# Sending half of a triangular solve's products to the other half of PSUM, in a fused delta-rule attention and MLP kernel

## The chip, the cores and the metric

The kernel runs on one core of a Trainium2 chip. The metric is the device time of one execution in microseconds; the times below are medians over several runs. A core has a matrix engine (TensorE, "PE"), three others that compute (VectorE "DVE", ScalarE "ACT", GpSimd "POOL"), a fifth that here only issues transfers (SyncE, "SP"), and 16 DMA engines. Each engine works through its own list of instructions in order; semaphores make one wait for another. Matrix products land in PSUM, which has 128 partitions and eight banks; DVE and ACT read them from there.

## The reference

There are 4 x 8 = 32 heads, 768 tokens and a head dimension of 48. Each head runs a delta rule over the tokens; the result goes through a two-layer MLP (384 to 2048 to 384) with a tanh Gelu.

```
k_n = k / (norm(k) + 1e-6)
for t in range(S):
    y[t]  = q[t] @ state
    state = state + beta[t] * outer(k_n[t], v[t] - k_n[t] @ state)
x = y with the heads side by side              # 3072 x 384
out = gelu_tanh(x @ w_in) @ w_out
```

## The kernel before

The 768 tokens are cut into 12 chunks of 64. Within a chunk the rule is a triangular system, so the work of a chunk c has these stages, each for all 32 heads at once. A "pair" p is two heads: one lies in partitions 0 to 63 of every tile, the other in 64 to 127, and there are 16 pairs.

- `prep(c)` squares the keys (`sq`), sums them (`ss`, L603) and forms 1/norm (`rn`). For chunks 0 to 3 the root is taken on ACT. From chunk 4 on it is taken for two chunks at once on DVE by a bit trick and three Newton steps (`norms`, L621 to L628: 12 small instructions). `prep2` multiplies keys by `rn` (`Kn`, POOL or DVE), transposes them on PE (L680) and copies the result into `KQT`. `prepq` does the same for the queries, two chunks at a time (L648).
- `gram` forms K K^T and K Q^T (`G`, `DT`). `own` forms the 16 x 16 diagonal blocks of K K^T, and `solve` inverts them on POOL (chunk 0: on DVE), in pairs of chunks from 2 on. `back` (L806) transposes the inverses into `TB`; `exp` spreads them over zero-padded tiles: `DI` (block diagonal) and `WB`.
- `inverse(c)` makes the inverse `TT` of the 64 x 64 triangle from the four diagonal blocks, by Horner's scheme. First `ET` = a product of `G` and `WB` ("WB,G" in the profile), masked. Then for k = 1, 2, 3: a product of `ET` with `DI` (k = 1) or with `TT` so far (k = 2, 3), 64 - 16k columns wide, and an addition of `DI` into `TT` on DVE. In the profile the products are "DI,ET" (64x48) and "TT,ET" (64x32, 64x16). Each is 32 matmuls with a 64 x 64 stationary tile, one for each head.
- `state(c)` computes v minus what the state already says (`R`), `U` = `TT` times `R`, the new state `S` and the chunk's rows of x.
- `mlp(t)` works on token tiles: chunks 0 to 3 are a tile each, then two chunks make a tile (eight tiles). Its first layer goes in blocks of one PSUM bank ("x,W"), each followed by a Gelu on ACT into `gT`; its second layer is "W,gT", evicted to `osb` and sent out.

All matmuls of attention and MLP stand on L267 (`f_mms`), all DVE and POOL two-operand operations on L251 (`f_tt`), copies on L256 (`f_cp`), most of ACT's on L260 (`f_act`), all DMA issues on L275 (`f_dma`).

A product with a 64 x 64 tile can read from either half of the partitions and write to either half. In the product WB,G of chunks 2 on, even pairs write to the half that they read from, and odd pairs to the other half and another bank (`flip` in `prod`). In the products of the loop over k, every pair writes to the half that it reads from.

Nothing is scheduled at run time or by a planner in this file. The string `ORDER` gives every operation, by its number in the order of creation and the letter of the engine that is to run it (v, a, g, p, s for DVE, ACT, POOL, PE, SP), in one sequence; each engine's list is its part of it, and an operation that can run on several engines is put on one by that letter. Words such as `w12.5` are 12 filler matmuls ("spins", L414) into bank 5. The string `BANK` gives the PSUM bank of each product. `BANKS` limits which banks a kind may have: 0 to 5 for attention ("t"), 6 and 7 for the MLP ("f"), any for the first chunks and the last tile ("l"). A product waits for every user of its bank's last tile.

Of the kernel before, what the change touches and what calls it, by code (L numbers as in the profile page):

```python
# [19 lines left out]
v33 v10 s56 v3 w6.7 p61 v36 v37 v9 v38 s51 v42 v7 v40 s52 a82 g84 v63 s60 a24 g20 v85 g17 a29 v39 v62 a30 a31 v83 a32  # L20
a23 v67 a86 s59 v70 a87 v64 v88 s57 a97 g75 v89 v65 g81 s58 w12.5 p91 v66 a98 p99 g90 v44 v92 g77 w1.4 p93 a103 v68
p100 v94 g72 g76 a101 s96 p152 v104 g74 v153 g73 a105 w1.7 p181 a106 a182 v107 v154 g108 v156 v155 g69 w8.3 p109 v157
v158 v159 a110 v160 v183 g80 s141 a102 v161 w4.5 p264 v162 v163 v164 p178 v265 a179 v165 g266 v166 a117 v167 v168 v169
v170 a25 a28 g267 a27 v171 g268 g269 v172 g270 g271 v173 g272 g273 v174 g274 g275 v175 g276 g277 v176 a185 g278 g279
s95 a184 v177 w29.3 p191 g280 p301 g281 v192 g282 a187 p189 v186 g283 v190 g284 a188 w1.5 p195 g285 v118 p193 g286
a196 g287 a194 p199 v71 g288 v180 p197 g289 a200 g78 a119 p203 v198 a120 g290 a205 p201 v121 g291 v204 v122 g79 a202
p209 a302 p206 g292 g293 s147 v207 a210 g294 g295 a125 v208 s140 v211 g296 w3.5 p215 v303 p216 g297 p217 s146 p304
v218 a219 p212 p123 v126 a305 g299 v298 a127 a128 v129 a133 v306 g130 v300 s115 v124 a213 s113 g400 w12.7 p131 v308
a309 s116 p398 v132 a311 s114 g603 v214 p399 a250 s111 p314 v401 a310 s112 a315 v251 s144 g402 s142 a375 v307 s143
g403 g404 w10.6 p312 v376 a135 s145 g405 p224 g406 s262 g407 p226 v377 a225 g408 v378 s263 v379 p328 a134 g409 v380  # L30
p228 v381 g410 v382 a313 s151 g411 v329 p136 g412 p137 s150 a229 g413 v383 p316 v138 p318 g414 s149 a317 v384 g415
p438 a227 v385 s223 p230 g416 v386 v139 a439 g417 s222 p232 a231 v387 g418 s148 v388 p320 a233 g419 v389 p459 v319
g390 s220 p234 a460 v440 s221 p322 a235 v321 p456 v461 p324 g420 a323 s396 a457 g393 p326 p441 s397 v327 a519 p236
v325 v458 p333 a442 g421 v520 p238 g422 a334 p391 g423 a253 v443 g424 p330 g425 a239 v331 p338 g426 p394 a252 v332
g427 v335 p339 v392 p340 g428 p341 a578 s259 p342 g429 p240 g430 v344 s260 g431 a343 g433 v579 a395 s258 p254 a237
g432 v580 p601 s345 v437 p602 s261 a444 v434 p241 s346 v462 s347 v604 p255 s348 a242 p349 s436 v256 g605 p351 a350
s435 v581 p644 v582 a352 p466 s531 v583 g521 p353 v584 a645 v585 s532 v445 p245 g522 a354 v646 a257 g606 v586 v587
g607 p355 g608 v464 a467 g609 p336 v588 v446 p448 g610 v337 p246 g611 a449 g612 v589 g613 v463 p523 g614 v590 a356
v591 p474 g615 v592 a247 p450 g690 a447 p357 v451 p359 v475 g593 p524 a360 p452 v525 a358 p468 g616 v453 a526 s599
p361 g596 v469 s600 p454 a362 p363 s527 v455 g617 v691 p476 s530 g618 p470 a477 g619 p480 s529 p594 g620 a364 p481  # L40
s528 g621 p478 a482 g622 p365 v479 s483 g623 a771 g624 s489 v471 p366 g625 s491 a595 v772 g626 s488 g627 g628 p533
a243 v773 s490 p662 v774 g629 p597 a244 v775 s492 g630 v776 p370 g631 a598 v777 s487 v778 g632 v779 g633 v780 s703
a367 g634 p371 v781 g636 v782 a692 s702 v783 v784 v785 g635 p794 v534 a372 a663 p795 v640 g786 a465 p493 v647 p495
v664 a494 g693 p472 v797 a496 p497 s792 g883 p499 v473 a498 s793 v637 p535 v648 s638 g796 p501 a536 v884 s699 p539
a502 p540 p641 g798 s486 v541 p694 a642 s639 p503 a500 v643 s700 g799 p695 a504 g800 p505 v696 g801 s548 p507 a506
s546 v697 p537 a665 s547 p651 g789 p659 v652 p509 s701 a508 s550 v538 a660 g802 p790 s549 g803 a374 p510 v661 g804
s698 a958 g805 v791 s551 g806 a249 v649 p837 g807 p669 v959 s484 p653 a248 g808 s485 p514 g809 a838 v654 g810 a668
g811 v670 a511 p515 g812 g813 v667 v839 g814 p552 g815 v960 a516 v961 p655 g816 v962 a553 p834 g817 v656 p677 a835
g818 p554 v963 g819 a650 v678 p556 g820 a555 g821 p657 v836 a557 g822 p558 v658 a886 g823 v666 g824 p679 g825 a559
p683 p671 g826 a680 g827 p560 g828 v672 p681 a561 p562 v682 g829 p673 a563 v830 p684 p704 v674 s832 a685 p564 v705  # L50
s545 p675 a565 s831 p852 v676 a369 p566 v964 s542 a853 v965 p710 v966 s544 p706 v967 a567 p568 v968 s543 v969 a707
v970 v841 a368 v854 p711 p855 v971 a712 p569 v860 v972 v859 g973 a856 v833 s719 p787 a373 v842 s720 p573 v857 a858
g885 s717 s721 p974 v840 a517 s722 p708 v788 p862 a570 g976 p574 s718 v863 a512 s688 v709 s687 g981 p864 a575 p977
s689 a576 v865 p887 s686 g1133 p888 v975 p723 v889 p844 a724 p725 v845 a861 p727 a843 v978 a726 p979 v890 a728 p980
p846 v982 p729 p731 v847 g983 a730 p1019 a732 p866 p1022 g984 v867 p848 g985 a1023 g986 p733 v849 g987 p735 g988 v1024
g989 p1131 a736 g990 g991 p1132 a734 g992 a1020 p737 g993 v1021 p739 g994 a738 g995 v1134 p870 a740 g996 p741 g997
p743 v871 a742 g998 g999 p850 a518 g1000 p868 a744 g1001 p745 v869 g1002 v851 p747 g1003 a746 g1004 p872 a748 p876
g1005 p749 a873 g1006 g1007 p751 a750 g1008 p874 g1009 a752 p877 g1010 v875 p753 a878 g1011 g1012 p1037 g1013 p891
a754 p755 v892 a577 g1135 a513 v1015 p897 a571 p893 s1016 g1014 p756 v894 a1038 s716 s715 g1136 v1018 g1137 p898 p1040
s714 g1138 a899 p759 g1139 s1017 v757 g1140 a1041 g1141 v1039 s713 p760 g1142 a572 v1043 s907 g1143 a1025 v1042 g1144  # L60
s906 p763 g1145 v1044 s904 v1026 g1146 a758 s908 g1147 v1045 v761 p1171 g1148 s905 p1029 a1172 p764 g1149 s909 a1028
g1150 v1173 s903 g1151 v1030 p767 g1152 a765 s881 g1153 v1027 s879 g1154 p1047 s882 g1155 p895 p1031 g1156 s902 p910
g1157 v1032 s880 g1158 p768 a911 g1159 v1048 g1160 g1161 p912 v896 g1162 g1163 p1174 g1164 a913 p1049 g1165 p1033 a769
v1050 a1175 p914 g1166 v1034 p916 a915 p1055 v1170 a917 p1051 p918 v1052 p920 v1177 a919 v1056 p1035 a921 p1053 a762
v1036 p922 v1176 p924 a923 p1057 a925 p926 v1058 a1046 p928 a927 v1195 p1061 a929 v1167 p1059 p1062 v1060 s1169 p930
a1063 s900 p932 v1054 a931 s901 p1068 p1074 a933 v1069 p1189 s1168 p934 a1190 p936 v1191 a935 p1070 a937 p938 v1071
a770 p940 a939 v1197 p1181 a941 v1179 p1075 p1192 v1196 a1076 p942 v1182 a766 s1080 p943 a1180 s1078 s1067 p946 v944
s1064 a945 s1065 p947 a1193 s1066 v1194 s1077 p950 v1178 a948 s1081 a949 s1079 p951 s1082 p1199 a952 p1072 p1183 a953
p954 v1184 v1200 p1083 p955 v1073 a1084 p1207 a956 p1213 v1208 p1185 p1085 v1186 p1087 p1201 a1088 p1187 a1086 p1089
v1188 a957 v1202 p1091 a1090 p1209 a1198 p1203 v1210 a1092 p1093 v1204 p1095 a1094 p1214 a1096 p1205 a1215 p1211 p1097  # L70
v1212 p1099 a1098 v1206 p1216 a1100 p1101 v1217 p1103 a1102 p1218 a1104 p1105 v1219 p1107 a1106 p1220 a1108 p1109
p1111 a1110 p1221 a1112 p1113 v1222 p1115 a1114 s1226 p1116 s1227 s1225 s1224 p1119 a1117 s1228 s1223 p1120 p1123
a1121 p1124 p1229 a1125 p1231 a1230 p1233 a1118 p1235 a1232 p1237 p1239 p1241 a1240 p1127 a1242 a1236 p1243 a1234
a1238 p1245 a1244 p1247 a1246 p1249 p1251 a1250 p1253 a1122 p1255 a1126 p1257 a1252 a1248 p1259 p1261 a1260 a1254
p1128 a1256 a1258 p1262 v1129 a1130 p1265 a1263 a1264 p1266 p1269 p1270 p1273 v1271 v1267 a1268 p1274 a1272 a1275
a1276
"""
BANK = ("6031340340660141100441256766766777042000503073120036766677667154142444144220200367676676760000276766"
        "7676754202240042244430024042067667677676767676767024104052244440000220220666767676767676767661042024"
        "2242042530200022767767667676767676764000444440000044210001203141021031450102")  # L80


# [1257 lines left out]
```

## Time and profile before

| | |
|---|---|
| median of 3 runs | 252.25 us |
| the runs | 252.25, 252.91, 249.76 us |
| span of the profiled execution | 249.4 us (its time is not listed apart) |
| PE busy | 232.0 us, 5637 matmuls |
| DVE, ACT, POOL busy | 161.4, 139.0, 118.6 us |
| DMA | 23.84 MB, mean 96 GB/s |

In the profile, "busy" is the time in which an engine had an instruction under way, and a row such as `108.03 0.68 PE ... x32` gives a group's start, its length and its number of instructions. Matmuls overlap, so the time that a group costs is read from its start to the start of the next. "Issue" is waiting for which no other engine is seen to be the cause. The chain that ended last is followed back from the last instruction to what released it each time.

### The profile page before, as it was taken

The numbers are of one execution on the slowest core, as the hardware profiler recorded it, in microseconds if no ns is written. First come the engines' busy times: TensorE is split into PE (matmuls) and PEld (weight loads), VectorE is DVE, ScalarE is ACT, GpSimd is POOL, SyncE is SP. The second block draws the span as 40 slices with busy tenths as digits, with TensorE's granted clock in tenths as the row PEclk, the third lists the DMA queues.
The fourth block names the chain that finished last, engine by engine and source line by source line (L and its number), as shares of the span: only waits on it lengthen the run. The fifth ranks groups of instructions, "written<-read, shape, count | busy, mean of one in ns | idle before, by whom it ended". The sixth has DMA issues, their size and how long they took to land.

```text
span 249.4 us, 12386 instructions
## 1 busy us (share of the span) xinstructions
PE 232.0 (93%) x5637; PEld 155.0 (62%) x5637; DVE 161.4 (65%) x316; ACT 139.0 (56%) x262; POOL 118.6 (48%) x249
## 2 busy tenths in 40 slices
PE   7577896998999799999899999999999999999995
PEld 4334473587778658868766655666656665555562
DVE  6699989886799399896969653767772465100001
ACT  2744578587686466838564357535682247426600
POOL 3685796688389858588045589883000000000000
PEclk9999999799999799999999999999999999999999
DMA  6999969996740825550244000623135210000112
GB/s 157 209 196 168 159 116 211 159 214 107 184 87 19 192 52 112 122 137 7 57 111 91 5 20 23 149 57 63 37 76 134 78 37 3 8 11 32 66 63 96
DMA packets 64789, 23.84 MB, mean 96 GB/s; under 512 B 53600, under 2 KB 63840, under 8 KB 64736
## 3 DMA queue, kind: packets, MB, share of 16 engines
q1 hardware_dynamic: 58656, 14.89, 30.8%
q0 software_dynamic: 1056, 3.15, 7.3%
q10 hardware_dynamic: 5024, 5.02, 6.3%
q8 instruction: 44, 0.72, 1.2%
q14 instruction: 9, 0.07, 0.1%
HBM read 20.64 MB, written 4.72 MB: 102 GB/s over the span
## 4 chain that ended last, share of the span: by engine, by line
PE 81%; DVE 10%; DMA 2%; issue 2%; ACT 2%; POOL 0%; ACTq 0%; POOLq 0%
PE ps L267 76%; DMA kf<-in_k_dram 2%; PE ps L648 2%; PE ps L680 2%; PE ps L414 1%; DVE ss L603 1%; DVE WB L931 1%; ACT WB L915 1%; DVE TB L806 1%; DVE KQT L256 1%; DVE ps L846 1%; DVE Yf L251 1%; DVE Tt L837 1%; DVE btz L251 0%; DVE ps L786 0%
## 5 line engine op out<-in xcount | busy, mean ns | idle before, releaser
L260 ACT ACTIVATE gT<-ps 128x512 bf16<-128x512 f32 x96 | 55.9, 597 | 38.4 <-PE ps L267 36.8
L267 PE MATMUL ps<-x,W 128*128 128x256 bf16 (+1 forms) x384 | 72.2, 329 | 0.0
L267 PE MATMUL ps<-W,gT 128*128 128x384 bf16 x384 | 67.0, 328 | 0.0
L267 PEld LDWEIGHTS ps<-W,gT 128*128 128x128 bf16 x384 | 36.4, 98 | 23.9 <-issue 0.5
L267 PEld LDWEIGHTS ps<-x,W 128*128 128x128 bf16 x384 | 39.1, 115 | 16.3 <-issue 0.3
L762 POOL TENSOR_TENSOR Yf<-Yf,tmp 128x28 f32<-128x28 f32 (+13 forms) x84 | 28.8, 342 | 6.4
L759 POOL TENSOR_TENSOR tmp<-Yf 128x28 f32<-128x28 f32 (+13 forms) x84 | 28.1, 335 | 6.1
L251 DVE TENSOR_TENSOR TT<-ps,DI 128x768 bf16<-128x768 f32 (+2 forms) x30 | 20.2, 684 | 13.8 <-PE ps L267 13.5
L414 PE MATMUL ps<-wz 128*128 128x512 bf16 x87 | 23.3, 416 | 1.4 <-DVE wz L409 1.4
L251 POOL TENSOR_TENSOR Kn<-kf,rn 128x768 bf16<-128x768 f32 (+1 forms) x11 | 16.0, 1452 | 17.1 <-DVE rn L629 10.1
L267 PE MATMUL ps<-KQT 48*32 48x32 bf16 (+1 forms) x1152 | 18.7, 195 | 5.8 <-issue 2.7
L260 ACT ACTIVATE osb<-ps 128x384 f32<-128x384 f32 x18 | 8.8, 490 | 26.3 <-PE ps L267 26.3
L256 DVE COPY osb<-ps 128x384 f32<-128x384 f32 x6 | 3.2, 552 | 29.8 <-PE ps L267 29.8
L260 ACT ACTIVATE G<-ps 128x512 bf16<-128x512 f32 x24 | 14.3, 597 | 11.4 <-PE ps L267 7.7
L267 PEld LDWEIGHTS ps<-KQT 48*32 48x32 bf16 (+1 forms) x1152 | 13.6, 95 | 10.9 <-issue 5.0
L719 DVE TENSOR_TENSOR DT<-ps,mD 128x512 bf16<-128x512 f32 x24 | 16.3, 680 | 4.1 <-ACT G L260 4.1
L267 PE MATMUL ps<-TT,ET 64*64 64x32 bf16 (+1 forms) x768 | 16.4, 176 | 0.0
L267 PEld LDWEIGHTS ps<-TT,ET 64*64 64x64 bf16 x768 | 14.8, 109 | 2.2 <-DVE R L251 0.6
L414 PEld LDWEIGHTS ps<-wz 128*128 128x128 bf16 x87 | 8.7, 105 | 11.5 <-issue 3.0
L251 DVE TENSOR_TENSOR S<-ps,S 128x768 bf16<-128x768 f32 x10 | 9.5, 953 | 9.0 <-PE ps L267 8.9
L260 ACT ACTIVATE x<-ps 128x1024 bf16<-128x1024 f32 (+2 forms) x10 | 9.2, 916 | 8.1 <-PE ps L267 7.9
L251 DVE TENSOR_TENSOR R<-ps,vf 128x768 bf16<-128x768 f32 x11 | 10.4, 949 | 3.8 <-PE ps L267 3.8
(122 smaller groups left out, 333.2 us busy)
## 6 DMA issues: line engine op xcount, KB each, us to landing
qf<-in_q_dram SPq DMA_DIRECT2D x24, 192.0 KB, 4.4
kf<-in_k_dram SPq DMA_DIRECT2D x23, 192.0 KB, 4.9
vf<-in_v_dram SPq DMA_DIRECT2D x40, 96.0 KB, 3.2
out_dram<-osb ACTq DMA_DIRECT2D x16, 192.0 KB, 2.0
W<-in_moe_w_out_dram POOLq DMA_DIRECT2D x4, 384.0 KB, 6.7
out_dram<-osb ACTq DMA_DIRECT2D x16, 96.0 KB, 2.8
W<-in_moe_w_in_dram POOLq DMA_DIRECT2D x4, 192.0 KB, 8.7
vf<-in_v_dram SPq DMA_DIRECT2D x4, 192.0 KB, 11.3
```

What stands on the lines that cost most here:

```text
L251: return lambda e: e.tensor_tensor(out() if callable(out) else out, a() if callable(a) else a, b() if callable(b) else b, op)
L256: return lambda e: e.tensor_copy(out, a() if callable(a) else a)
L260: return lambda e: e.activation(out, a() if callable(a) else a, func)
L267: ins = t.matmul(out, lhsT, rhs, start=st, stop=sp_, skip_group_check=skip)
L414: ins = e.matmul(psum[:, b, :], wz[:, 0:128], wz[:, :], start=True, stop=True)
L603: op({"dve": 0.95 * w}, {"dve": lambda e, u=u: e.tensor_reduce(ss[j][:, u], sq[:, u, :], AX.X, ALU.add)}, reads=[f"sq{n}"], writes=[f"ss{j ...
L648: ins = e.transpose(o[:, a, j], Qn[:, n, a, j, :, :].rearrange("q h d -> q (h d)"), identB[:, :])
L680: ins = e.transpose(tb()[:, m, :], t[:, 2 * m:2 * m + 2, :].rearrange("p h d -> p (h d)"), identB[:, :])
L719: op(d_ps(512), {"dve": lambda e: e.tensor_tensor(dv, gview(1)(), md, ALU.mult)}, reads=[h] + MD, writes=[dn])
L759: sop(nb * s * w, lambda e, s=s, w=w, tv=tv: e.tensor_tensor(tv, yf[:, :, s:s + 1, 0:s].to_broadcast([128, nb, w, s]), Yv()[:, :, s + 1:16 ...
L762: sop(nb * s * w, lambda e, s=s, tv=tv: e.tensor_tensor(Yv()[:, :, s + 1:16, 0:s], Yv()[:, :, s + 1:16, 0:s], tv, ALU.add), [YN, TN], [YN])
L806: op({"dve": 0.58}, {"dve": lambda e: e.transpose(dst, src)}, reads=reads, writes=writes)
```

## The change

There are four parts.

1. For chunks 4 to 11 (`CX = 4`) the three products of the loop over k send odd pairs to the other half of the partitions and to a second bank, so a product takes two banks for each k (before: two for k = 1, one for k = 2 and 3). The addition on DVE becomes three instructions, each half as wide: even pairs over 128 partitions, then the odd pairs' two halves, each read from one half and written to the other.
2. For chunks 4 and 5 the root of the norms and the addition of 1e-6 are done on ACT (two instructions) and not on DVE (12). The reciprocal stays on DVE.
3. `BANKS` lets every kind of product use every bank, and `BANK` is new.
4. `ORDER` is new in most places. The number of spins stays 87; 37 operations go from DVE to ACT and 25 from ACT to DVE, five from POOL to ACT and three from ACT to POOL.

```diff
-BANKS = {"t": (0, 6), "f": (6, 8), "l": (0, 8)}
+BANKS = {"t": (0, 8), "f": (0, 8), "l": (0, 8)}
 GATE = 2
+CX = 4
...
-v34 a50 g11 s49 v5 v0 g21 v46 a48 s47 g22 v6 g16 v8 v35 v41 g18 s54 v1 v4 a2 g13 g14 s55 g12 g19 v15 v45 s53 a26 v43
...
+v0 g11 s49 a50 g21 v34 v5 v46 w6.0 g22 a48 s47 g16 v6 g18 v8 v35 v41 g13 v4 v1 s54 a2 g14 g12 g19 v15 s55 v45 v43 v33
...
-                norms(lambda e: e.tensor_scalar(y_.bitcast(I32), s_.bitcast(I32), -0.5, 1597463007.0, op0=ALU.mult,
-                                                op1=ALU.add), sn_, yn_)
-                for _ in range(3):
...
+                if c < 6:
+                    op({"act": 0.24}, {"act": f_act(a_, s_, ACT.Sqrt)}, reads=sn_, writes=["nw"])
+                    op({"act": 0.21}, {"act": lambda e: e.activation(a_, a_, ACT.Copy, bias=1e-6)}, reads=["nw"], writes=["nw"])
+                else:
...
-                    op({"pe": 0.467 * w}, bk="l" if c < 2 else "t", fns={"pe": prod(hk, ET[e_], src[:, :, 16 * k - off:64 - off], n, per, g)},
...
+                    if c < CX:
...
+                    def place(p, hk=hk, n=n):
+                        return bank(hk, p % 2)[:, n * (p // 2):n * (p // 2) + n]
+
+                    def cross(src=src, off=off, k=k, place=place):
+                        return [(place(p)[HALF[a ^ (p % 2)], :], ET[e_][HALF[a], p, :], src[HALF[a], p, 16 * k - off:64 - off],
+                                 True, True, True) for p in range(NP) for a in range(2)]
+
+                    def add(e, hk=hk, n=n, k=k, cols=cols):
+                        for par, o_, i_ in ((0, slice(0, 128), slice(0, 128)), (1, HALF[0], HALF[1]), (1, HALF[1], HALF[0])):
+                            ins = e.tensor_tensor(TT[r_][o_, par::2, cols],
+                                                  bank(hk, par)[i_, 0:8 * n].rearrange("q (p t) -> q p t", t=n),
+                                                  DI[r_][o_, par::2, 16 * k - 16:48], ALU.add)
+                        return ins
...
+                       writes=[hk], alloc=[(hk, 2)])
```

More of the change, by code (lines that the diff above doesn't have):

```diff
@@ L22 @@
[L22 to L56, printed above, removed]
@@ new lines @@
+s145 g393 w5.6 v315 g394 g395 s262 v309 g134 a225 a378 a135 s263 g396 p136 g397 p328 g398 p318 g399 s143 v329 p137
+a319 g400 s148 a229 g401 p230 v138 a313 g402 s151 p236 g403 v139 a231 s150 g404 v379 p316 g405 s142 p428 g383 p322
+a317 s149 p446 a323 p320 a429 p326 v321 a237 g380 v430 a327 p431 a447 p226 a509 v448 g406 s387 p449 p381 a450 g407
+v510 s386 p333 a227 g408 p324 v451 a432 g409 p234 s223 g410 a325 v433 a253 p232 g411 v334 g412 a235 p384 v382 g413
+a233 p238 g414 v385 a335 a252 g415 p338 p330 g416 a568 s258 p254 g417 g418 p255 s220 a239 g419 p240 g420 v256 a331
@@ new lines @@
+s222 g421 g422 a332 v569 a257 p339 s261 p591 g423 v424 s221 p340 p341 p592 v570 s259 g786 v427 p336 p342 s260 v594
+p241 a343 s425 a344 v337 a434 g595 s426 p349 v242 s347 p351 v571 a350 g596 v572 g597 v573 s348 a452 p634 p438 g598
+p464 g599 s345 v439 p355 g600 a352 s522 g601 v465 g512 p456 a356 p353 a511 g602 v574 p245 g603 v575 a354 s519 v453
+g604 a437 v576 v435 g605 s346 a457 v436 g606 v577 p440 s521 g607 p246 v441 s518 g608 g609 v578 g610 v579 p442 a247
+v454 g611 v580 p513 a249 g612 v443 s476 a635 p514 g613 v581 a455 s474 p444 v582 a515 g583 p458 s475 v445 p357 v459
@@ new lines @@
+a248 a516 g614 p359 s589 v636 g615 a358 s590 p460 g616 p466 g617 v461 p361 g618 a467 s520 g619 p470 a680 g620 s517
+g621 a360 g622 v681 p471 g623 a362 p468 g624 g586 p363 v472 p365 a364 v469 g625 s480 a244 a761 p652 p366 g626 a653
+v762 s481 s479 v627 p587 a367 s477 v630 p462 a588 s478 v763 p584 v463 p370 v764 s482 a585 v765 v654 v766 v767 a243
+s693 v768 p784 a682 v769 v638 p785 s629 v770 s628 p523 p371 v524 s473 v787 p525 a372 p485 a683 v771 v656 g788 p491
+v526 s690 p529 a492 s692 v772 g789 v773 p530 a373 g790 v774 p631 s689 p684 g791 a632 v775 v637 g792 p483 a486 v639
@@ L83 @@
+p1264 a1257 a1258 p1260 v1265 a1266 a1261 a1262
+"""
+BANK = ("6031325540664245232363644532154255336072525372076201001453420040032035612225400623334000320561027023"
+        "5630743666110066444460044011147067057271142067024021663210635532325055553732020571570776035060153150"
+        "0350353355515361225677627655174306235203216364402044036317064770251425114672")
 class Op:
@@ L620, in prep @@
                 yn_ = [f"sr{d % 2}" for d in pair]
-                norms(lambda e: e.tensor_scalar(y_.bitcast(I32), s_.bitcast(I32), -0.5, 1597463007.0, op0=ALU.mult,
-                                                op1=ALU.add), sn_, yn_)
-                for _ in range(3):
+                if c < 6:
+                    op({"act": 0.24}, {"act": f_act(a_, s_, ACT.Sqrt)}, reads=sn_, writes=["nw"])
+                    op({"act": 0.21}, {"act": lambda e: e.activation(a_, a_, ACT.Copy, bias=1e-6)}, reads=["nw"], writes=["nw"])
+                else:
+                    norms(lambda e: e.tensor_scalar(y_.bitcast(I32), s_.bitcast(I32), -0.5, 1597463007.0, op0=ALU.mult,
+                                                    op1=ALU.add), sn_, yn_)
+                    for _ in range(3):
+                        norms(f_tt(a_, y_, s_, ALU.mult), sn_ + yn_, ["nw"])
+                        norms(lambda e: e.scalar_tensor_tensor(a_, a_, -0.5, y_, ALU.mult, ALU.mult), yn_ + ["nw"], ["nw"])
+                        norms(lambda e: e.scalar_tensor_tensor(y_, a_, 1.5, y_, ALU.add, ALU.mult), yn_ + ["nw"], yn_)
                     norms(f_tt(a_, y_, s_, ALU.mult), sn_ + yn_, ["nw"])
-                    norms(lambda e: e.scalar_tensor_tensor(a_, a_, -0.5, y_, ALU.mult, ALU.mult), yn_ + ["nw"], ["nw"])
-                    norms(lambda e: e.scalar_tensor_tensor(y_, a_, 1.5, y_, ALU.add, ALU.mult), yn_ + ["nw"], yn_)
-                norms(f_tt(a_, y_, s_, ALU.mult), sn_ + yn_, ["nw"])
-                norms(lambda e: e.tensor_scalar(a_, a_, 1e-6, None, op0=ALU.add), ["nw"], ["nw"])
+                    norms(lambda e: e.tensor_scalar(a_, a_, 1e-6, None, op0=ALU.add), ["nw"], ["nw"])
                 op({"dve": 0.25}, {"dve": lambda e: e.reciprocal(rn2[:, z, :], a_)},
@@ L1011, in inverse @@
                         continue
-                    op({"pe": 0.467 * w}, bk="l" if c < 2 else "t", fns={"pe": prod(hk, ET[e_], src[:, :, 16 * k - off:64 - off], n, per, g)},
-                       nm=int(32 * w), reads=nm(sn, y) + nm(f"ET{e_}", y) + ([f"DI{r_}e"] if fl else []), free=nm(f"TT{r_}b", y),
-                       writes=[hk], alloc=[(hk, max(1, int(NP * w) // per))])
-                    op(d_ps(16 * n * w), {"dve": f_tt(two(TT[r_][:, :, cols], per, g), view(hk, n, per, g),
-                                                      two(DI[r_][:, :, 16 * k - 16:48], per, g), ALU.add)},
+                    if c < CX:
+                        op({"pe": 0.467 * w}, bk="l" if c < 2 else "t", fns={"pe": prod(hk, ET[e_], src[:, :, 16 * k - off:64 - off], n, per, g)},
+                           nm=int(32 * w), reads=nm(sn, y) + nm(f"ET{e_}", y) + ([f"DI{r_}e"] if fl else []), free=nm(f"TT{r_}b", y),
+                           writes=[hk], alloc=[(hk, max(1, int(NP * w) // per))])
+                        op(d_ps(16 * n * w), {"dve": f_tt(two(TT[r_][:, :, cols], per, g), view(hk, n, per, g),
+                                                          two(DI[r_][:, :, 16 * k - 16:48], per, g), ALU.add)},
+                           reads=[hk] + nm(f"DI{r_}", y) + ([f"DI{r_}e"] if fl else []), writes=nm(f"TT{r_}b", y))
+                        continue
@@ L1017, in inverse @@
+                    op({"pe": 0.274}, {"pe": f_mms(cross)}, bk="t", nm=32,
+                       reads=nm(sn, y) + nm(f"ET{e_}", y) + ([f"DI{r_}e"] if fl else []), free=nm(f"TT{r_}b", y),
+                       writes=[hk], alloc=[(hk, 2)])
+                    op({"dve": 3 * (0.10 + 1.06e-3 * 8 * n)}, {"dve": add},
                        reads=[hk] + nm(f"DI{r_}", y) + ([f"DI{r_}e"] if fl else []), writes=nm(f"TT{r_}b", y))
```

65 lines of the change are left out of this document (40 added, 25 removed).

## The prediction

> **What bounds the kernel now.** I read the page first, then the stretches of time, then the chain that ended last.
>
> ```profile
> span 249.4 us, 12386 instructions
> PE 232.0 (93%) x5637; PEld 155.0 (62%) x5637; DVE 161.4 (65%) x316; ACT 139.0 (56%) x262; POOL 118.6 (48%) x249
> ```
>
> ```profile
> 45.00:60.00 15.00, 14.28 (x308) 10.89 (x307) 12.79 (x31) 10.81 (x23) 12.48 (x26) 0.94 1.00 177
> 60.00:75.00 15.00, 14.53 (x441) 11.40 (x440) 11.90 (x27) 11.52 (x23) 9.64 (x22) 1.00 0.52 115
> ...
> 105.00:120.00 15.00, 15.00 (x459) 11.61 (x459) 12.31 (x23) 9.19 (x17) 11.71 (x30) 1.00 0.27 65
> 120.00:135.00 15.00, 14.25 (x430) 10.38 (x418) 12.13 (x27) 7.39 (x13) 6.29 (x5) 1.00 0.42 94
> 135.00:150.00 15.00, 14.34 (x531) 9.46 (x520) 9.79 (x13) 8.02 (x16) 9.12 (x23) 1.00 0.11 24
> ```
>
> ```profile
> 44.35 3.42 PE ps L414 x10
> ...
> 143.45 0.62 issue
> 144.07 102.42 PE ps L267 x2080
> ```
>
> Columns of the middle fence: PE, weight loads, DVE, ACT, POOL, granted clock, DMA share, GB/s. From 45 us on PE is busy 95 to 100% of each stretch, and the chain runs on PE without a break from 144.07 to 246.5. Up to 43 us the chain is on DVE and ACT instead: the first chunks' serial solve. So a microsecond of PE work saved after 45 us is worth up to a microsecond, and DVE or ACT work costs nothing as long as its queue keeps up. In 45 to 75 us it hardly does: DVE is busy 24.7 of 30 us, ACT 22.3.
>
> **The products (24 of them: chunks 4 to 11, k = 1, 2, 3).** The price stands in PE's timeline, since the WB,G product of the same loop already sends odd pairs to the other half.
>
> ```profile
> 107.78 0.42 PE L267 MATMUL ps<-WB,G 64*64 64x48 bf16 x32
> 108.03 0.68 PE L267 MATMUL ps<-DI,ET 64*64 64x48 bf16 x32
> 108.64 2.77 PE L267 MATMUL ps<-W,gT 128*128 128x384 bf16 x16
> ...
> 130.22 0.42 PE L267 MATMUL ps<-WB,G 64*64 64x48 bf16 x32
> 130.57 1.47 PE L267 MATMUL ps<-W,gT 128*128 128x384 bf16 x8
> ```
>
> From start to next start, 32 matmuls of DI,ET take 108.64 - 108.03 = 0.61 us. The 32 of WB,G take 108.03 - 107.78 = 0.25 us when 64x64 work follows, and 130.57 - 130.22 = 0.35 us when a full-array product follows. Before a full-array product an edit saves 0.61 - 0.35 = 0.26 us. Before other 64x64 work the old form already overlaps: of the TT,ET group at 121.15, 28 matmuls had started when the next group began at 121.59, so 0.44 us; the saving is 0.19. Bounds: 24 x 0.19 = 4.6 and 24 x (0.61 - 0.25) = 8.6 us. In the new order about half are followed by each kind; I take 0.25 each, **-6.0 us** on PE.
>
> **The adds behind them (DVE).** One TENSOR_TENSOR over 128 partitions becomes three of half the columns: even pairs, then odd pairs' two halves crosswise.
>
> ```profile
> L251 DVE TENSOR_TENSOR TT<-ps,DI 128x768 bf16<-128x768 f32 x10 | 9.5, 945 | 7.4 <-PE ps L267 7.4
> L251 DVE TENSOR_TENSOR TT<-ps,DI 128x512 bf16<-128x512 f32 x10 | 6.9, 686 | 2.3 <-PE ps L267 2.2
> L251 DVE TENSOR_TENSOR TT<-ps,DI 128x256 bf16<-128x256 f32 x10 | 4.1, 421 | 4.1 <-PE ps L267 3.9
> ...
> L256 DVE COPY osb<-ps 128x384 f32<-128x384 f32 x6 | 3.2, 552 | 29.8 <-PE ps L267 29.8
> ```
>
> No row shows an add on 64 partitions; I price it by its columns per partition. 384 columns: 0.55 us by the COPY row. 256: 0.42. 128: 0.29 (CAST TT 128x128 at 32.67 us in DVE's timeline). End to end that is 3 x (0.55 + 0.42 + 0.29) = 3.78 us against 2.05, +1.7 per chunk and 13.8 in all. Instructions in a row overlap, though: two 768-column adds took 1.55 us (170.68), not 1.89. With about 0.08 us hidden in each, it is +1.2 per chunk, 9.8 in all. I take 9.8; the other end is 13.8. The cover: these products lie between 105 and 210 us, where the stretches give DVE 70.0 of 105 us busy, so 80 to 84 still fits: **0 on the path**. If the cover failed at every step, PE would stand the full 9.8.
>
> **The norms of chunks 4 and 5.** Twelve small DVE instructions go; by their rows (sr 0.18, four nw products of 0.26, three of 0.31, three of 0.26, the last add 0.50) that is 3.4 us, stretched in the trace from 48.02 to 54.25. ACT gets a root and a biased copy at 0.22 each (the sr rows at 32 us), 0.44. The new root stands in ACT's order before the second table load, so the loads stay two; but the load (1.28 us, at 38.02 in a quiet ACT) now waits for DVE's sum of chunk 5. That sum stands behind the transpose of chunks 2 and 3 (44.04, 1.25 us) and takes 0.95, so about 46.3; root, load and warm-up bring the first Gelu to about 48. In the trace it ran at 48.95, so the wait is hidden. Behind it in ACT's queue stand the Q copies, TT evictions and Gelus of tile 0; half of Q's copy goes to POOL, behind three solve steps, ready at about 48.4. So state work of chunk 1 (49.50 before) cannot come much before 49.
>
> **The order.** The spins (L414) are 87 in both, but ten move ahead of chunk 0's inverse, where DVE and ACT set the pace anyway (WB, G at 28.22), and 16 instead of 26 stay between chunk 0's inverse and chunk 1's state. The ten at 44.35 took 3.42 us. Two first-layer blocks of tile 0 move ahead of chunk 1's inverse; the second half of chunk 4's keys no longer stands on SP behind chunk 5's first half, which waits until DVE has read chunk 2's keys (about 34 us), and their square goes to POOL. Chunk 1's two WB (2.6 us at 39.9 on DVE, 1.0 at 46.05) go to ACT. Bounds: +1.0 (POOL's Q copy late, and ACT's queue late with it) to -3.4 (all ten spins' time); I take **-1.5**, nearer the lower half since 49 us is a floor for state 1.
>
> **The shared banks.** MLP blocks had two banks of their own, now any of eight. Comparing, in the new order, the PE work between a tile's product and the reuse of its bank with the eviction's row, I find eight or so tight places after chunk 1 (tile 2's last first-layer blocks: 0.56 us of PE work against a Gelu of 0.60). Each is short by 0.1 to 0.2 us: **+1.0**, bounds 0 and 3. Engine moves (37 evictions or expansions from DVE to ACT, 25 back, five from POOL to ACT, three the other way) are 0 while the queues keep up.
>
> **Sum:** -6.0 - 1.5 + 1.0 + 0.2 (more semaphores behind the longer adds) = -6.3 us. The profiled span is 249.4, the fastest timed run 249.76, so at most 0.4 lies around it; the median is 2.85 above the span, and I carry that along: 243.1 + 2.85 = **246.0 us**. Ends: -8.6 - 3.4 = -12.0 and -4.6 + 1.0 + 3 = -0.6, so this case's own range is 240.5 to 251.6.
>
> **Rivals.** (1) *The longer adds set the pace in chunks 4 to 7.* The loop is serial: product, add, product, add. For it: DVE is busy 12.1 to 12.3 of 15 us in 105 to 135. Against: between chunk 4's k = 1 and k = 2 the new order puts a half second-layer product (1.31), a WB,G (0.3) and a Gram (0.3), 1.9 us, against 1.5 for the add; elsewhere more. If half of the 9.8 us is uncovered, -6.3 + 4.9 = -1.4: **250.8 us**. The Trainium skill (TensorEngine Tiling (Array Packing), Performance Considerations, "PSUM Bottleneck") warns of just this: tiling makes TensorE faster and leaves the emptying of PSUM as it was, which may then be the bottleneck. By that rule this rival's time holds; the trace agrees so far as WB,G takes 0.25 us and its eviction 0.95.
>
> (2) *ACT's queue stalls the shared banks: slower.* ACT takes 16 instructions more, the roots included (at its mean of 139.0 / 262 = 0.53 us some 8.5 us), and every late eviction now holds a bank that a state product may want. If a Gelu stands behind a 1.02 us KQT copy at one in eight of the 96 Gelus, PE waits 12 times: -6.3 + 12.2 = +5.9, **258 us**. It decides from six such waits (gain gone) and eleven (slower by 2%). For it: ACT at 11.5 of 15 us in 60 to 75. Against: Gelus waited 36.8 us for PE, so ACT is mostly the one that waits.
>
> (3) *The quadrants do not overlap:* products stay at 0.61, about 252 us. WB,G speaks against.
>
> **Chances.** Forecast 0.58, rival 1 0.22, rival 2 0.18, rival 3 0.02. A measurement of this kernel can tell about 2% (5.0 us) from no change. Of the forecast 0.56 lies below 247.2, of rival 1 0.02: faster 0.58. Within 2%: 0.02 + 0.20 + 0.02 = 0.24. Slower: 0.18. The range goes from 241.0, near the forecast's lower end, to 256.0, past rival 1 and short of rival 2's centre.
>
> **What would show it.** Right: 32 TT,ET matmuls at 0.25 to 0.36 us from start to start in chunks 4 on; PE's busy time down by about 6; DVE's within 4 of 161 (+9.8 for the adds, -3.4 for the norms, and twelve instructions net to ACT at its mean of 0.51); the last unbroken PE run of the chain still some 95 us long; first Gelu near 48 us. Rival 1 shows as PE waits on DVE TT of over a microsecond between 100 and 160 us; rival 2 as PE waits on ACT gT, KQT or x. The prediction is wrong if PE's busy time does not fall, or falls and the chain leaves PE after 60 us.

## The result and the profile after

The changed kernel takes 250.73 us (median of 20 runs, 246.29 to 253.66); the kernel before, in 20 runs of the same comparison, 251.71. The ratio is 0.9846, with a 95% interval of 0.9806 to 0.9885. Ratios in this document use only the fast runs, those within 1.5% of the same kernel's fastest, which here are 7 of the 20 after and 17 of the 20 before, so that this ratio is lower than that of the two medians, 0.996. Two further comparisons of the unchanged pair gave 0.9944 (0.9908 to 0.998) and 0.9923 (0.9875 to 0.9972). So by the ratios the change gains 0.6 to 1.5%, some 1.4 to 3.9 us; by the medians of all runs the three comparisons give 1.0, 2.1 and 1.8 us. 6.3 us had been forecast. The mean granted clock varies from run to run (0.952 to 0.993 in the 20 runs after), and time goes with it: a straight line through these 20 runs falls by 1.35 us for each 0.01 (253.66 us at 0.952; 246.29, 246.37 and 249.0 at 0.993). In the traces a lower mean is made of stretches of 3.4 us or more at half clock, two before (from 43.2 and 84.2 us) and three up to 180 us after (from 11.1, 38.4 and 69.1). The profiled runs had 0.986 before and 0.979 after, so their spans are not compared to the last microsecond here.

The page's head of the changed kernel:

```profile
span 248.9 us, 12428 instructions
PE 229.8 (92%) x5637; PEld 151.5 (61%) x5637; DVE 160.9 (65%) x335; ACT 143.5 (58%) x277; POOL 115.9 (47%) x247
```

PE's busy time fell by 2.2 us, its idle time rose from 17.4 to 19.1. DVE's busy time stayed, since what the adds put on it left elsewhere. The stretches (columns as before: PE, weight loads, DVE, ACT, POOL, clock, DMA share, GB/s):

```profile
45.00:60.00 15.00, 13.60 (x353) 10.51 (x345) 9.54 (x16) 12.64 (x31) 11.88 (x24) 1.00 0.85 168
60.00:75.00 15.00, 13.84 (x448) 10.51 (x449) 9.33 (x17) 9.67 (x21) 10.97 (x26) 0.89 0.59 125
...
105.00:120.00 15.00, 14.87 (x461) 11.02 (x460) 14.68 (x26) 9.03 (x15) 11.60 (x25) 1.00 0.47 94
120.00:135.00 15.00, 14.89 (x464) 10.82 (x462) 13.99 (x36) 8.94 (x16) 3.46 (x3) 1.00 0.34 74
135.00:150.00 15.00, 14.79 (x479) 9.73 (x479) 10.84 (x19) 9.84 (x18) 11.32 (x25) 1.00 0.15 34
150.00:165.00 15.00, 13.91 (x438) 8.58 (x437) 10.11 (x18) 7.91 (x14) 13.12 (x37) 1.00 0.17 39
165.00:180.00 15.00, 14.31 (x433) 8.47 (x432) 13.18 (x27) 7.87 (x14) 3.29 (x8) 1.00 0.36 84
```

DVE went from 12.3 and 12.1 us to 14.7 and 14.0 in 105 to 135 us: nearly full, and yet PE is busy 14.9 of 15 us there. PE loses more from 150 to 180 us, where it had been busy 15.0 of 15 us in both stretches before. The products in PE's timeline (start, length):

```profile
110.11 0.43 PE L267 MATMUL ps<-TT,ET 64*64 64x32 bf16 x32
110.47 2.77 PE L267 MATMUL ps<-W,gT 128*128 128x384 bf16 x16
113.17 0.42 PE L267 MATMUL ps<-TT,ET 64*64 64x16 bf16 x32
113.45 0.42 PE L267 MATMUL ps<-DI,ET 64*64 64x48 bf16 x32
```

From start to next start 0.36 us ahead of a full-array product and 0.28 ahead of other 64x64 work; over all 24 products it is 0.25 to 0.46 us where PE did not wait, 0.35 on average, against 0.57 before. The chain that ended last (start, length, what; the longest unbroken PE piece was 102.42 us from 144.07 before):

```profile
145.47 1.25 DVE Tt L879
146.72 0.03 issue
146.75 0.42 DVE TT L1034
...
177.43 68.55 PE ps L267 x1165
```

The adds (L1034) now stand on the chain here and at 170 to 175 us. That looks like rival 1 of the prediction. PE's waits from 52 to 180 us (total, times, longest) say otherwise:

```profile
PE ps L267 <- ACT gT L260: 0.5, 1, 0.5
PE ps L267 <- DVE DI L928: 0.4, 1, 0.4
PE ps L267 <- DVE TT L1034: 0.2, 1, 0.2
```

PE itself waited 0.2 us for an add, once, and its weight loads 1.0 us in three waits. The rest of the 1.8 us that PE lost from 150 to 180 us is put down to other engines (0.4) or to nothing that the profile shows (issue, 1.1), which leaves open how much of it goes back to the adds. The chain walks back through whatever released the next step; it doesn't tell whether PE had other work to do meanwhile. Which of the two readings is right needed experiments.

### The profile page after: what moved, and what is told of

Same layout as the page of the kernel before. It is cut to its first block, busy times and chain, and to the rows that moved or that the text cites. A ratio compares the mean times of both kernels' runs of the same rounds, so it can differ in the third digit from the quotient of the medians.

```text
span 248.9 us, 12428 instructions
## 1 busy us (share of the span) xinstructions
PE 229.8 (92%) x5637; PEld 151.5 (61%) x5637; DVE 160.9 (65%) x335; ACT 143.5 (58%) x277; POOL 115.9 (47%) x247
## 4 chain that ended last, share of the span: by engine, by line
PE 74%; DVE 14%; ACT 4%; issue 3%; DMA 2%; POOL 2%; ACTq 0%; DVEq 0%; POOLq 0%
PE ps L267 67%; PE ps L652 3%; DMA kf<-in_k_dram 2%; DVE TT L1034 2%; PE ps L684 2%; PE ps L414 2%; DVE DT L723 1%; DVE DI L928 1%; POOL sq L251 1%; DVE R L251 1%; DVE Kn L251 1%; DVE ss L603 1%; DVE ET L251 1%; ACT DI L919 1%; ACT WB L919 1%
## 5 line engine op out<-in xcount | busy, mean ns | idle before, releaser
L260 ACT ACTIVATE gT<-ps 128x512 bf16<-128x512 f32 x96 | 53.7, 603 | 28.3 <-PE ps L267 28.0
L267 PE MATMUL ps<-W,gT 128*128 128x384 bf16 x384 | 68.6, 329 | 0.6 <-issue 0.6
L267 PEld LDWEIGHTS ps<-W,gT 128*128 128x128 bf16 x384 | 36.3, 98 | 24.8 <-issue 1.3
L267 PEld LDWEIGHTS ps<-x,W 128*128 128x128 bf16 x384 | 40.1, 116 | 18.0 <-issue 0.3
L1034 DVE TENSOR_TENSOR TT<-ps,DI 64x384 bf16<-64x384 f32 (+5 forms) x72 | 30.3, 421 | 8.3 <-PE ps L267 7.5
L251 POOL TENSOR_TENSOR Kn<-kf,rn 128x768 bf16<-128x768 f32 (+1 forms) x11 | 16.1, 1474 | 17.4 <-DVE rn L633 15.8
L260 ACT ACTIVATE KQT<-ps 128x1024 bf16<-128x1024 bf16 x15 | 15.2, 1022 | 9.6 <-PE ps L684 7.5
L267 PE MATMUL ps<-KQT 48*32 48x32 bf16 (+1 forms) x1152 | 18.0, 194 | 2.3 <-issue 1.1
L603 DVE TENSOR_REDUCE ss<-sq 128x16 f32<-128x768 f32 (+1 forms) x13 | 11.4, 875 | 4.6 <-POOL sq L251 3.1
L684 PE MATMUL ps<-identB,Kn 128*128 128x128 bf16 x96 | 8.5, 235 | 5.0 <-DVE Kn L251 4.0
L251 POOL TENSOR_TENSOR Yf<-Tt,bM 128x512 f32<-128x512 f32 x5 | 6.5, 1309 | 14.0 <-DVE nw L629 7.0
L267 PEld LDWEIGHTS ps<-TT,ET 64*64 64x64 bf16 x768 | 10.9, 108 | 3.5 <-issue 0.7
```

What stands on the lines that cost most here:

```text
L251: return lambda e: e.tensor_tensor(out() if callable(out) else out, a() if callable(a) else a, b() if callable(b) else b, op)
L260: return lambda e: e.activation(out, a() if callable(a) else a, func)
L267: ins = t.matmul(out, lhsT, rhs, start=st, stop=sp_, skip_group_check=skip)
L603: op({"dve": 0.95 * w}, {"dve": lambda e, u=u: e.tensor_reduce(ss[j][:, u], sq[:, u, :], AX.X, ALU.add)}, reads=[f"sq{n}"], writes=[f"ss{j ...
L684: ins = e.transpose(tb()[:, m, :], t[:, 2 * m:2 * m + 2, :].rearrange("p h d -> p (h d)"), identB[:, :])
L1034: ins = e.tensor_tensor(TT[r_][o_, par::2, cols], bank(hk, par)[i_, 0:8 * n].rearrange("q (p t) -> q p t", t=n), DI[r_][o_, par::2, 16 * k ...
```

## Experiments

All ratios are to the kernel before, run side by side with it. Experiments 1, 2 and 3 were measured in one set of runs, the others and the repeats in two later sets. New order means the changed kernel's order, banks and norms.

**1. The old products in the new order.**

```diff
-CX = 4
+CX = 12
```

> The changed kernel with every chunk's Horner products and adds in the old form (odd pairs in their own half, one add for each k); order, banks and norms as changed. Theory (each crosswise product is worth about 0.25 us of TensorE's time, and the three unhidden 64- and 128-partition adds, 3.79 us a chunk against 2.05, put VectorE on the path and give 2 to 3 us of it back): PE busy rises by 6 us or more, DVE busy falls by 13 to 14 us (to about 147), the last unbroken PE run of the chain of waits is over 95 us long again, and the time is 3 to 4 us above the changed kernel's, so about the kernel before's or up to 1.5 us above it (ratio 0.998 to 1.006), since the new order's start was later by 1.3 us. Rival 1 (longer adds eat the whole gain, and the order made the time shorter): the same time as the changed kernel within 1 us (0.981 to 0.988), or less. Rival 2 (the products' gain is all there is and the adds cost nothing): 6 us above the changed kernel, ratio 1.008 or more.

1.0057 (1.0019 to 1.0094). As the theory expected: order, banks and norms alone cost 0.57%, 1.4 us (0.5 to 2.4). The groups of PE by form in this kernel:

```profile
L267 PE MATMUL ps<-DI,ET 64*64 64x48 bf16 x384 | 8.4, 186 | 0.3 <-DVE ET L251 0.2
L267 PE MATMUL ps<-TT,ET 64*64 64x32 bf16 x384 | 8.3, 180 | 0.0
L267 PE MATMUL ps<-TT,ET 64*64 64x16 bf16 x384 | 8.2, 173 | 0.0
```

Together 24.9 us of PE (24.8 in the kernel before); in the changed kernel the same three are 6.6 + 6.5 + 6.3 = 19.4. So 24 crosswise products save 5.5 us of PE, 0.23 each.

**2. One wide add, and again.** The crosswise products stay; one add over both banks takes the place of three, so the odd pairs' numbers stay in the wrong half.

```diff
-    for par, o_, i_ in ((0, slice(0, 128), slice(0, 128)), (1, HALF[0], HALF[1]), (1, HALF[1], HALF[0])):
-        ins = e.tensor_tensor(TT[r_][o_, par::2, cols], bank(hk, par)[i_, 0:8 * n]..., DI[r_][o_, par::2, ...], ALU.add)
+    return e.tensor_tensor(TT[r_][:, :, cols].rearrange("q (p b) t -> q b p t", b=2),
+                           banks2(hk)[:, :, 0:8 * n].rearrange("q b (p t) -> q b p t", t=n),
+                           DI[r_][:, :, ...].rearrange("q (p b) t -> q b p t", b=2), ALU.add)
```

> The changed kernel with the three adds of each k made one over both banks, 128 partitions wide; it leaves out that the odd pairs are brought back to their own half, so those numbers end in the wrong half. Crosswise products, order, banks and norms as changed. Theory (the three adds cost 13.9 us of VectorE, of which 2 to 3 us lie on the path): DVE busy falls by 13 to 14 us to about 147, the adds take about 2.1 us a chunk, and the time falls by 2 to 3 us below the changed kernel's: ratio to the kernel before 0.973 to 0.978. Rival 1 (what is missing of the products' 6 us is eaten by the shared banks, ScalarE or the later start): within 0.7 us of the changed kernel, 0.982 to 0.988. A fall of 4 us or more (under 0.970) would say that the adds ate more than the whole difference to the forecast.

> The changed kernel with one wide add for each k, which leaves out that the odd pairs are brought back to their own half; again, now in one call with the unchanged version, so that the price of the three adds can be read from two ratios to the same runs of the kernel before. If the adds cost 1.5 to 2 us in the new order, this one is 0.6 to 0.8% below the unchanged version; if the order hides them, within 0.3%.

0.9907 (0.9865 to 0.9948), then 0.9878 (0.9832 to 0.9923) with 0.9923 for the changed kernel beside it. DVE's busy time fell by 15 us, from 160.9 to 145.9. The time fell by 0.45%, about 1.1 us, in the set that has both kernels, with intervals that overlap: anything from nothing to about 2.5 us fits. Over all sets the changed kernel's mean is 0.9904 and this one's 0.9893, 0.3 us apart. So my expectation of 2 to 3 us was probably too high: in the new order the adds are hidden but for 0.3 to 1.1 us, as the two ways of comparing have it. Against the old products in the same order (1.0057), the crosswise products alone are worth 1.5%, 3.8 us, in the same set (give or take 1.4), and 1.8%, 4.5 us, with the repeat, of the 5.5 us that PE saves.

**3. The same change in the old order.** The kernel before with crosswise products and three adds in chunks 4 to 8, 10 and 11; attention may use any bank, and four of the 276 bank numbers differ.

```diff
+    if c < 4 or c == 9:
         ... old products and add
+        continue
+    ... place, cross and add as in the change
```

> The kernel before with the crosswise products and their three adds alone, in chunks 4 to 8, 10 and 11 (in chunk 9 the old order leaves no two neighbouring banks free for k = 2 and 3); order, norms and all other banks as before. Theory: 21 products at 0.25 us less take 5 to 6 us from PE busy, DVE busy rises by 12 us to 173, and as the old order does not know of the longer adds, they cost as much as in the new order or more: 1 to 4 us below the kernel before, ratio 0.984 to 0.996. Rival 1 (in this order the adds set the pace in chunks 4 to 8): no gain or a loss, 0.998 to 1.010. Rival 2 (adds hidden): 5 us less or more, under 0.981.

1.0177 (1.0107 to 1.0246): the crosswise products and their adds by themselves make the kernel 4.4 us slower. PE's two largest waits in it from 52 to 180 us, and the weight loads' largest for another engine (in this file the adds are L1028):

```profile
PE ps L265 <- DVE TT L1028: 3.9, 5, 1.5
PE ps L265 <- DMA x<-x: 1.9, 2, 1.7
```

```profile
PEld ps L265 <- DVE TT L1028: 6.4, 8, 1.7
```

This is rival 1, and more than its range (up to 1.010), in an order that was made for the shorter adds: five PE waits for adds, the longest 1.5 us, where the kernel before had PE waits for no other engine in this stretch. The waits for a DMA of x, also new, come on top.

**4. One wide add in the old order.** Experiment 3 with the edit of experiment 2.

> The kernel before with the crosswise products of chunks 4 to 8, 10 and 11 in the old order, as in the run that was 1.0177 of the kernel before, but with one 128-partition add over both banks for each k in place of three; it leaves out that the odd pairs are brought back to their own half. Theory (in the old order the longer adds set the pace: PE waited 3.9 us and the weight loads 6.4 us for them): VectorE's busy time falls by 12 us to about 162, PE busy stays near 230, the waits for the adds go, and the time is 8 to 10 us below that run's, 0.978 to 0.988 of the kernel before. Rival (that run's loss came from the neighbouring banks, which the old order gives to its handles only just in time): less than 4 us of it comes back, 1.000 or more.

0.998 (0.9945 to 1.0015), against 1.0177. So in the old order the three adds cost 2.0%, 4.9 us (give or take 2, as the two ratios come from two sets); in the new order 0.3 to 1.1. The other half of the expectation failed: even with cheap adds the old order makes next to nothing of PE's saved time, 1.4 us at the most by the interval (0.978 to 0.988 was expected). Where it goes there is open; the neighbouring banks, free only just in time, are one candidate. In the one profile of this kernel (of an execution of 253.22 us) PE waits from 52 to 180 us for adds (1.1 us), for a DMA of x (1.0), for `R` (0.7), for evictions to `osb` (0.6), for Gelus (0.5) and for `G` (0.2), where the kernel before had no wait for an engine.

**5. Where the gain comes from, by chunks.** Crosswise products only in some chunks, new order.

```diff
-CX = 4
+CX = 8                       # chunks 8 to 11;  10: chunks 10 and 11
...
-                    if c < CX:
+                    if c < CX or c > 7:      # with CX = 4: chunks 4 to 7
```

> The changed kernel with the crosswise products and split adds in chunks 8 to 11 alone; chunks 4 to 7 in the old form. Order, banks and norms as changed. Theory (each crosswise product takes 0.23 us from PE's busy time in whatever chunk, and the new order hides the adds): 12 products less, PE busy 2.7 us above the changed kernel's, DVE busy 7 us below, and the time midway between the old products in this order (1.0057) and the changed kernel (0.985): 0.993 to 0.998. Rival 1 of the forecast (the adds of chunks 4 to 7 set the pace there): the time is at or below the changed kernel's. Rival (the gain lies in the early chunks alone, since PE has slack late): at the time of the old products, 1.002 or more.

> The changed kernel with the crosswise products and split adds in chunks 4 to 7 alone, the other half of the run with chunks 8 to 11 alone (0.994). Theory (in 105 to 135 us VectorE is busy 14.7 and 14.0 of 15 us, so there the longer adds take back what the products give): no gain over the old products in this order, ratio 1.002 to 1.008, though PE busy falls by 2.7 us. Rival (a crosswise product is worth the same in every chunk and the adds are hidden): 0.993 to 0.998, like the late half.

> The changed kernel with the crosswise products and split adds in chunks 10 and 11 alone, where VectorE has room (9 of 15 us busy from 180 us on). Theory (late products are worth their whole 0.23 us, six of them 1.4 us): 0.6% below the old products in this order, ratio 0.998 to 1.002. Rival (the gain of the late half came from chunks 8 and 9): 1.004 or more.

| crosswise products in | how many | ratio | below 1.0057 by |
|---|---|---|---|
| none | 0 | 1.0057 (1.0019 to 1.0094) | |
| chunks 10, 11 | 6 | 1.0001 (0.996 to 1.0043) | 0.6% |
| chunks 8 to 11 | 12 | 0.994 (0.9908 to 0.9973) | 1.2% |
| chunks 4 to 7 | 12 | 0.9973 (0.992 to 1.0027) | 0.8% |
| chunks 4 to 11 | 24 | 0.9846, 0.9944, 0.9923 | 1.1 to 2.1% |

The early half gains too, by these figures, against my expectation of nothing: 2.1 us for 12 products, 0.18 each, against 0.24 in the late half. The intervals of 0.9973 and 1.0057 just overlap, and 1.0057 is of another set, so the early gain is likely and not certain, and the two halves can't be told apart. If it holds, DVE's 14 to 14.7 busy us of 15 in 105 to 135 us take little from it. Nor can it be said whether the two halves add up in full.

**6. The start.** Chunk 4's square behind chunk 3's scaled keys on POOL's queue, and the eight early spins in bank 3.

```diff
-... w8.0 ... g250 ... g130 ...
+... w8.3 ... g130 g250 ...
```

> The changed kernel with two places of its start put otherwise: the square of chunk 4 stands behind the scaled keys of chunk 3 on GpSimd's queue, not ahead of them, and the eight spins that were in bank 0 (the bank in which chunk 0's block solve lies) are in bank 3 as before. Theory (these two made the start late): VectorE's 1.23 us wait for PE at about 18 us goes, GpSimd's scaled keys of chunk 3 begin 0.5 us earlier, the first product of state 1 comes 0.5 to 1.3 us earlier than 50.80 and the time falls by 0.3 to 1 us (ratio 0.981 to 0.984). Rival (the start waits for loads and the granted clock, and later waits take up what is won): state 1 within 0.3 us and time within 0.3 us of the changed kernel (0.984 to 0.986).

> The changed kernel with the square of chunk 4 behind the scaled keys of chunk 3 on GpSimd and the eight early spins in bank 3, again, in more rounds and beside the unchanged version of the same call. Theory (the start costs 0.5 to 1 us): 0.3 to 1 us below the changed kernel, ratio 0.980 to 0.985. Rival (later waits take it up): within 0.3 us of the changed kernel of this call.

0.9876 (0.9787 to 0.9965), then 0.993 (0.9888 to 0.9973) with 0.9944 for the changed kernel beside it: no difference that can be told. State 1 came at 51.67 us, not earlier than the 50.98 of the unchanged kernel, but this profile has one more stretch at half clock ahead of it (from 45.1 us). Chunk 3's transposes did come 1.0 us earlier (42.24 against 43.25), but the transpose of the blocks of chunks 2 and 3, which waits for chunk 4's square and sum in DVE's queue, came 0.6 us later (46.02 against 45.40). And the wait for the spins cost nothing that can be seen: without it the instruction itself takes longer. First the unchanged kernel, then this one, in DVE's timeline:

```profile
18.09 0.43 DVE L850 TENSOR_TENSOR ps<-Tt 128x256 f32<-128x256 f32 x1 [1.23 <-PE ps L414]
```

```profile
16.55 1.58 DVE L850 TENSOR_TENSOR ps<-Tt 128x256 f32<-128x256 f32 x1
```

What sets the end of the write in both is, by the times, GpSimd. The scaled keys (`Kn`) that run beside it on POOL end at 18.19 us in the first profile and at 17.84 in the second, and the write ends 0.33 and 0.29 us later, at 18.52 and 18.13. In all 14 profiles the write ends 0.29 to 0.34 us behind the POOL instruction beside it. No run moved the POOL instruction to test this.

**7. The unchanged kernel beside the repeats.**

> The changed kernel once more, as it is, beside the other runs of this chip, since two profiles of kernels that differ by 1 us can't be told apart by spans taken on different days. Every theory expects 1 to 2% below the kernel before (0.980 to 0.990). If the kernel with one wide add had been faster by the adds' cost, this one lies 1 to 3 us above its 0.9907 and thus near 1.000; if the new order hides the adds (PE waited 0.2 us for them at line 1034 in 52 to 180 us), it lies at 0.985 to 0.990.

> The changed kernel as it is, for the comparison with the one wide add and with the two parts. From its two earlier ratios (0.9846 and 0.9944): 0.985 to 0.995. If the chunks from 8 on carry the whole gain, it equals the run with chunks 8 to 11 alone (0.994).

0.9944 and 0.9923, used above; 0.9944 lies between the first expectation's two marks, 0.990 and 1.000. Within the intervals the run with chunks 8 to 11 alone equals it; no version that computes the same can be told to be faster.

## Why the prediction was off, step by step

The time, 250.73 us, lies in the range of 241 to 256, 4.7 above the forecast of 246.0, and at rival 1's 250.8; that it falls on this figure is chance, as the adds have at most a small part in it. It is faster, as forecast, but by less than the 2% for which the chance of 0.58 stood. By the prediction's own terms:

| term | forecast, us | measured, us | from |
|---|---|---|---|
| products, PE's busy time | -6.0 | -5.5 | groups of PE |
| products, in time | -6.0 | -3.8 to -4.5 | experiment 2 against 1 |
| adds, DVE work | +9.8 | +13.9 | groups of DVE |
| adds, on the path | 0 | +0.3 to +1.1 (up to 2.5 by the interval) | experiment 2 |
| order -1.5, banks +1.0, norms 0, semaphores +0.2 | -0.3 | +1.4 (0.5 to 2.4) | experiment 1 |

In time the measured terms add up to -1.3 to -2.8 us, which overlaps with the gain of 1.4 to 3.9. Every one of them missed in the same direction. Of the signs that the prediction had set, the price of a product and DVE's busy time (160.9, within 4 of 161) came as expected. PE's busy time fell by 2.2 us and not by about 6, the last unbroken PE piece is 68.55 us and not some 95, and the sign of being wrong, a chain that leaves PE after 60 us, appeared at 145 and 170 us, though PE's waits for adds there are short.

**Products.** The price was read rightly: 0.36 and 0.28 us against the 0.35 and 0.25 of WB,G. The step that failed is "a microsecond of PE work saved after 45 us is worth up to a microsecond", used as worth a whole one. With the adds out of the way too, some 1.0 to 1.7 of the 5.5 us are missing from the time: in the first one-add profile PE is busy 4.9 us less than with the old products (228.2 against 233.1, both at a clock of 0.986), and idle 1.0 us more (18.9 against 17.9). With the old products PE is busy 1.1 us more in the new order than in the old (233.1 against 232.0), which, with the lower clock of its profile, may be why the changed kernel's PE time fell by only 2.2; why the new order has more of it is open.

**Adds.** The columns priced the half-wide instructions well (0.55, 0.42, 0.29). The overlap of 0.08 us in each did not come. The row from which it was read merges two forms: the two adds at 170.68 have 768 and 512 columns (0.96 us, and 0.68 from 171.56), so 0.08 us was hidden and not the 0.34 that two adds of 768 would mean. The groups by form:

```profile
L1034 DVE TENSOR_TENSOR TT<-ps,DI 64x384 bf16<-64x384 f32 x16 | 8.9, 554 | 0.2
L1034 DVE TENSOR_TENSOR TT<-ps,DI 64x256 bf16<-64x256 f32 x16 | 6.8, 422 | 0.2
L1034 DVE TENSOR_TENSOR TT<-ps,DI 64x128 bf16<-64x128 f32 x16 | 4.6, 288 | 0.2
L1034 DVE TENSOR_TENSOR TT<-ps,DI 128x384 bf16<-128x384 f32 x8 | 4.4, 556 | 2.8 <-PE ps L267 2.7
```

Half the partitions cost as much as all (554 and 556 ns for 384 columns). Six adds in a row, of 256 and 128 columns, took 2.22 us in the changed kernel; their means add up to 3 x 0.42 + 3 x 0.29 = 2.13, so nothing was hidden. In the one-add kernel two adds in a row, of 512 and 256 columns, took 0.98, and their means are 0.69 + 0.42 = 1.11:

```profile
146.75 2.22 DVE L1034 TENSOR_TENSOR TT<-ps,DI 128x256 bf16<-128x256 f32 x6
```

```profile
147.05 0.98 DVE L1033 TENSOR_TENSOR TT<-ps,DI 128x512 bf16<-128x512 f32 x2
```

The Trainium skill has the rule (VectorE: DVE Perf Modes, "Two Vector instructions with no wait between them"): an instruction that starts to read or write a memory in another group of 32 partitions than the last one did there begins only when all earlier ones of VectorE have finished. The second and third add do just that, and the trace agrees; by this rule the prediction should have taken its upper end of 13.8, and 13.9 was measured. That it made so little of the time is the new order's work: the 0 on the path was nearly right, but its reason (DVE's free time) was not enough, since the old order offers the same free time and pays about 4.9 us.

**Order, banks, norms.** Together they came out with the wrong sign, and the record points in the main to the start, which the order arranges. The profiles of the kernel before and of experiment 1 have the same clock, 0.986; from 52 to 180 us PE waits 3.7 and 3.9 us in them, while state 1 comes at 49.50 and 50.51, which is 1.0 of the 1.6 us between their spans (249.4 and 251.0). State 1 was forecast not much before 49 us, so earlier than 49.50 if anything; in the changed kernel it came at 50.80, and in the ten other profiles of this order between 49.72 and 53.97. The clock makes much of this spread. Where a single stretch of about 3.4 us at half clock lies ahead of state 1, the old order has it at 49.50 and 49.35, the new one at 49.72, 50.51 and 51.47. The forecast's bound for this term, the 3.42 us of ten spins at 44.35, was itself read in such a stretch (granted clock 0.51 from 43.2 to 46.6): there the spins start 0.43 us apart, at full clock 0.21, and eight of them took 1.90 us at 14.81.

Two moved operations that the forecast did not follow stand inside the serial solves of chunks 0 and 1. DVE's timeline, before and in the changed kernel:

```profile
22.07 0.18 DVE L786 TENSOR_TENSOR ps<-ps,tmp 128x12 f32<-128x12 f32 x1
...
22.44 0.69 DVE L793 TENSOR_TENSOR Tt<-Yf,ps 128x512 f32<-128x512 f32 x1
```

```profile
23.21 0.18 DVE L790 TENSOR_TENSOR ps<-ps,tmp 128x12 f32<-128x12 f32 x1
23.44 0.71 DVE L580 TENSOR_SCALAR nbT<-nbT 128x192 f32<-128x192 f32 x1
...
24.08 0.67 DVE L797 TENSOR_TENSOR Tt<-Yf,ps 128x512 f32<-128x512 f32 x1
```

From the solve's last small step to its first large one 24.08 - 23.21 = 0.87 us, against 22.44 - 22.07 = 0.37 before: the negation of `nbT` (at 31.0 us before, 0.24 long) costs the chain 0.5 us. It takes 0.71 us here since, as the times have it, it runs beside a multiplication on POOL (22.77 to 24.04) and ends 0.12 us behind it, as in the ten other profiles of this order. With the negation done early, POOL can scale blocks (`bM`) at 26.01, for 1.26 us, in the middle of chunk 1's solve; before, it did so after the solve, at 39.79. The first key load took 6.11 us against 5.68, but in the profiles of this order it ranges from 5.56 to 6.87, so nothing can be put down to it. Putting the two operations back was not tried, so that they make up the 1.4 us is argued, not shown; nor were the banks and the norms priced apart.

**Norms, table load.** The root ran at 47.50 (forecast 46.3 for the sum), the load from 47.74, the first Gelu at 49.15 against 48.95 before: 1.1 us later than the forecast's 48, but near its cover.

**The sum's frame.** In every run that has both, time is 1.7 us or a little more above the span; the prediction held it to at most 0.4 and carried 2.85. It started from a median of three runs, 252.25; the kernel before's 20 runs have 251.71. From that base the same sum gives 245.4, and the miss is 5.3 us and not 4.7: about 0.5 us of it was hidden by luck. The lower end of the case's own range is 252.25 - 12.0 = 240.25 by its terms, not 240.5.

**Rivals 2 and 3.** PE's waits for ACT's Gelus were 0.5 us from 52 to 180 us, so rival 2 did not occur. Rival 3 is refuted by the 0.28 and 0.36 us.

## What to carry to other kernels

A step that is shorter on the bound engine and longer on its partner is worth what the order makes of it: nearly the same edit (chunk 9 aside) gave +1.8% in the order made for the old lengths, and in one made for the new -0.6 to -1.5% with the cost of that order in it. Price the two apart by a run that keeps the gain and leaves the cost out, and don't take an instruction on the chain for a cost until such a run, or the bound engine's wait for it, shows it. And follow every moved operation into the serial stretch that it now stands in, small ones on idle engines too.

## What was not expected of the hardware

- An add over 64 partitions takes as long as one over 128 with the same columns (554 and 556 ns), and adds whose partition halves alternate run end to end.
- A VectorE instruction that adds two tiles of SBUF may last as long as a GpSimd instruction beside it. The sum of two halves of `Tt` into `Yf` behind the write of experiment 6 took 1.48 or 1.49 us beside POOL's `bM` and ended 0.28 us behind it in 12 profiles; in the two in which `bM` was over, it took 0.41. So a wait that vanishes may reappear as duration: the write took 0.43 us after a 1.23 us wait for the spins, or 1.58 us without one, and the next instruction began 2.2 us after the start of the one ahead in both cases (18.43 - 16.23 and 18.05 - 15.89).
